# A fused softmax convolution and token mixer on one core: how the first load of x, the later loads, the zeros and the order of work are changed

## The chip, the cores and the metric

One core of one Trainium2 chip runs one program. The time is device microseconds of one launch, from the unprofiled runs; a separate profiled execution gives the trace. TensorE is PE in the profile (PEld its weight loads), VectorE is DVE, ScalarE is ACT, GpSimd is POOL, SyncE is SP. Loads and stores of the core share 16 DMA engines.

## What is computed

The input x has shape (8, 4224, 192) in fp32: 8 batches, 4224 tokens, 192 channels, in 8 heads of 24 channels. Two steps follow each other.

```python
# step 1: causal convolution over 7 tokens, one softmaxed filter per head
w = softmax(weight, axis=-1)                      # (8, 7)
y[b, s, h] = sum_k w[h, k] * x_pad[b, s + k, h]   # 6 zero rows ahead of each batch
# step 2: token mixing without a softmax, then an output projection
wq, wk = y @ w_q, y @ w_k                         # 192 -> 64 each
mixed  = (wq @ wk.T / 8) @ y                      # per batch, over all 4224 tokens
out    = relu(mixed) @ w_out                      # 192 -> 192, fp32
```

Since step 2 has no softmax, the kernel never forms the 4224 x 4224 matrix: it builds the Gram matrix y.T @ y of a batch (192 x 192), multiplies it with w_k, and applies the result to wq.

## The kernel before

**Tiles.** A batch is cut into 35 chunks (`NCC`) of 122 tokens (`CW`); a chunk is loaded as 128 rows, with the 6 tokens ahead of it. `XW` holds the chunks of all 8 batches in bf16 at once, so no load waits for a buffer. `Y`, `WQT` and the mixing weights `MSB`, `MBD` have two buffers; `RT` (relu results) has 3 and `OUT` (fp32 results, from which stores go) has 4.

**Stages of a batch**, each made by a function that adds operations to a list: `gen_conv` (matmuls of `XW` with the band matrix `BAND`, L391/L392, evacuated into `Y` at L671), `gen_transpose` and `gen_transpose_hi` (tokens to the free side, L395/L396 and L726), `gen_wq` (L751/L755), `gen_gram` (L787), `gen_mix_weights` (the small products behind a batch's Gram matrix), and `gen_mix` (mix_lo L878, mix_hi L890, relu L907/L908, fin_hi L935, fin_lo L391/L392 on `WOL`, evacuation L970, store L978 by SP). Most matmuls use 64 columns of the array and run in pairs side by side; mix_lo and fin_hi use 64 rows instead.

**Order.** `Planner.plan` takes the operations and simulates five engines with given durations; whenever an engine is free it places the ready operation with the lowest turn from the list `TURNS`, one number per operation. `STAY` is added to the turn of an operation that would change PE between 64 columns and 64 rows, and `HOLD` is how long PE waits for one that doesn't. The outcome is a fixed instruction stream for every engine, in which each instruction waits for semaphores; `tail` and `lands` tell the planner when a transfer is taken to have landed.

**The start.** DVE sets some tiles to zero (`zero_w` to `zero_m`, L410 to L422), POOL makes the identity, SP loads the 8 x 7 filters (L402). DVE then runs the chain of the softmax: wmx (L461), two subtractions, the exponential on ACT (L482), sum, reciprocal, `wtap`, `taps` (L494). PE spreads `taps` into PSUM in two halves of 512 columns, and ACT and DVE each evacuate one half into `BAND` (L527). The first convolution waits for both halves, for x, and for `zero_x`, `zero_x0`.

**Loads.** All loads of x go through POOL's queue, which turns fp32 into bf16 on the way (L565). Batch 0 comes in groups of 9, 9, 9 and 8 chunks, the later ones in groups of 18 and 17; a group is one large transfer, and the first and the last chunk of a batch have one of their own. POOL issues them one after the other without waiting for any landing. The mixing weights go by SP's queue (L587), behind the landing of the second group.

Of the kernel before, what the change touches and what calls it, by code (L numbers as in the profile page):

```python
# [13 lines left out]
    int(t) / 1000  # L14
    for t in """
# [56 lines left out]
class Op:  # L72


    n = 0
# [983 lines left out]
```

## Time and profile before

| what | value |
|---|---|
| median of 3 runs | 177.69 us (177.29 to 178.58) |
| the profiled execution's own time | 177.53 us |
| its span, first to last instruction | 175.7 us |
| PE busy | 157.1 us (89%), 3226 matmuls |
| ACT busy, DVE busy | 123.5 us (70%), 118.0 us (67%) |
| POOL's queue (loads of x) | 36128 packets, 13.61 MB |
| SP's queue (filters, weights, stores) | 12000 packets, 26.31 MB |
| instruction queue | 25 packets, 0.41 MB |

A line of the page's groups reads: line, engine, operation, tiles out<-in, shapes, count | busy time, mean of one in ns | idle time of the engine just before, and what ended it. In the timeline the columns are start, duration, engine, line, operation, tiles, shapes, count, and in brackets the idle time before with its releaser. "issue" as a releaser means that nothing which the profile shows was waited for. A line of waits reads: who waited, for whom, us in total, times, the longest. The bytes of POOL's queue are counted as written, in bf16.

### The profile page before, as it was taken

The page shows a single profiled execution, that of the slowest core. Times are in us where ns is not written, and L with a number is a line of the kernel's source. Part 1 is how long each engine was busy: PE and PEld are TensorE (multiplying, and loading weights), DVE is VectorE, ACT ScalarE, POOL GpSimd, SP SyncE. Part 2 cuts the span into 40 slices and gives each one's busy share as a digit, 9 for nine tenths or more (in the row PEclk, how much of TensorE's full clock was granted, in tenths as well). Part 3 has the DMA queues.
Part 4 walks back from the last instruction along what each step waited for, and adds up shares of the span by engine and source line. Part 5 has one row for each costly group of instructions (what it writes and reads, how often), then busy time and mean ns, then how long its engine had stood idle before and what let it go on. Part 6 is the DMA issues. An engine that isn't in the chain of part 4 may idle for free.

```text
span 175.7 us, 7099 instructions
## 1 busy us (share of the span) xinstructions
PE 157.1 (89%) x3226; PEld 121.7 (69%) x3226; DVE 118.0 (67%) x216; ACT 123.5 (70%) x206; POOL 30.3 (17%) x39
## 2 busy tenths in 40 slices
PE   0289799888999999899989979999999999999990
PEld 0179666776787787668778766878767777877550
DVE  6556587765766677586787738689688675765740
ACT  3243677597787948668648747888888896698980
POOL 7999452524230000000000000000000000000000
PEclk9999999999999999999999999999999999999995
DMA  3999999999999999999999999067283045987787
GB/s 30 162 189 186 205 191 193 191 196 277 193 279 194 286 309 268 343 250 243 304 264 282 237 194 348 24 244 297 103 343 127 4 175 216 356 347 309 265 303 262
DMA packets 48157, 40.36 MB, mean 230 GB/s; under 512 B 37632, under 2 KB 40960, under 8 KB 48128
## 3 DMA queue, kind: packets, MB, share of 16 engines
q0 software_dynamic: 36128, 13.61, 65.1%
q1 hardware_dynamic: 12000, 26.31, 40.9%
q8 instruction: 25, 0.41, 0.9%
q14 instruction: 4, 0.03, 0.1%
HBM read 27.56 MB, written 25.95 MB: 305 GB/s over the span
## 4 chain that ended last, share of the span: by engine, by line
PE 88%; issue 4%; DVE 3%; ACT 2%
PE ps L391 25%; PE ps L787 14%; PE ps L935 8%; PE ps L392 7%; PE ps L395 6%; PE ps L726 6%; PE ps L878 5%; PE ps L751 4%; PE ps L890 4%; PE ps L755 4%; PE ps L396 3%; ACT rt L907 1%; ACT out_sb L970 1%; DVE band L527 0%; DVE xw L416 0%
## 5 line engine op out<-in xcount | busy, mean ns | idle before, releaser
L970 ACT COPY out_sb<-ps 128x768 f32<-128x768 f32 (+1 forms) x46 | 34.7, 768 | 15.1 <-PE ps L392 11.3
L671 ACT CAST y<-ps 122x816 bf16<-122x816 f32 (+3 forms) x46 | 35.7, 791 | 13.2 <-PE ps L392 12.8
L907 ACT ACTIVATE rt<-ps 128x1024 bf16<-128x1024 f32 (+3 forms) x44 | 34.1, 800 | 6.4 <-PE ps L878 4.5
L787 PE MATMUL ps<-y 122*64 122x192 bf16 (+4 forms) x840 | 33.8, 222 | 2.2 <-issue 2.2
L970 DVE COPY out_sb<-ps 128x768 f32<-128x768 f32 (+1 forms) x26 | 21.6, 840 | 19.7 <-PE ps L392 18.5
L392 PE MATMUL ps<-wol,rt 128*64 128x192 bf16 x264 | 33.9, 255 | 1.0 <-issue 1.0
L787 PEld LDWEIGHTS ps<-y 122*64 122x64 bf16 (+1 forms) x840 | 31.1, 112 | 4.9 <-issue 2.8
L565 POOL DMA_DIRECT2D xw<-in_x_dram x34 | 29.9, 893 | 22.3 <-issue 21.5
L391 PE MATMUL ps<-wol,rt 128*64 128x192 bf16 x264 | 33.7, 255 | 0.0
L391 PE MATMUL ps<-xw,band 128*64 128x432 bf16 (+3 forms) x144 | 31.8, 335 | 1.5 <-DVE band L527 0.9
L392 PE MATMUL ps<-xw,band 128*64 128x432 bf16 (+3 forms) x144 | 32.1, 337 | 1.1 <-issue 1.1
L391 PEld LDWEIGHTS ps<-wol,rt 128*64 128x64 bf16 x264 | 24.1, 138 | 8.1 <-issue 2.0
L908 DVE TENSOR_SCALAR rt<-ps 128x512 bf16<-128x512 f32 (+3 forms) x36 | 23.6, 674 | 8.2 <-PE ps L878 7.6
L671 DVE CAST y<-ps 122x864 bf16<-122x864 f32 (+3 forms) x26 | 23.6, 912 | 8.0 <-PE ps L392 7.5
L698 DVE COPY ytl<-ps 128x976 bf16<-128x976 bf16 (+1 forms) x40 | 23.0, 591 | 3.9 <-PE ps L396 3.3
L392 PEld LDWEIGHTS ps<-wol,rt 128*64 128x64 bf16 x264 | 24.1, 138 | 1.2 <-issue 1.2
L396 PE MATMUL ps<-ident,y 122*64 122x122 bf16 x280 | 21.1, 219 | 0.0
L395 PE MATMUL ps<-ident,y 122*64 122x122 bf16 x280 | 21.0, 219 | 0.0
L935 PE MATMUL ps<-woh,rt 64*128 64x192 bf16 x264 | 20.4, 250 | 0.2 <-ACT rt L907 0.2
L395 PEld LDWEIGHTS ps<-ident,y 122*64 122x64 bf16 x280 | 18.1, 112 | 2.0 <-issue 0.5
L726 PE MATMUL ps<-ident,y 122*64 122x122 bf16 (+1 forms) x344 | 17.1, 220 | 1.3 <-DVE y L671 0.7
L396 PEld LDWEIGHTS ps<-ident,y 122*64 122x64 bf16 x280 | 17.7, 112 | 0.0
(95 smaller groups left out, 218.8 us busy)
## 6 DMA issues: line engine op xcount, KB each, us to landing
out_dram<-out_sb SPq DMA_DIRECT2D x28, 768.0 KB, 5.1
xw<-in_x_dram POOLq DMA_DIRECT2D x7, 816.0 KB, 33.2
xw<-in_x_dram POOLq DMA_DIRECT2D x7, 768.0 KB, 33.7
out_dram<-out_sb SPq DMA_DIRECT2D x8, 384.0 KB, 3.3
xw<-in_x_dram POOLq DMA_DIRECT2D x2, 432.0 KB, 8.3
out_dram<-out_sb SPq DMA_DIRECT2D x8, 96.0 KB, 4.3
xw<-in_x_dram POOLq DMA_DIRECT2D x1, 384.0 KB, 5.2
xw<-in_x_dram POOLq DMA_DIRECT2D x8, 45.8 KB, 25.0
```

Source lines behind the costliest of these rows:

```text
L391: e.matmul(out[0:64], lhsT[:, 0:64], rhs, **k)
L392: return e.matmul(out[64:128], lhsT[:, 64:128], rhs, **k)
L395: e.transpose(out[0:64], in_[:, 0:64], identity)
L396: return e.transpose(out[64:128], in_[:, 64:128], identity)
L565: lambda e, op, part=part: e.dma_start(*part),
L671: return e.copy(dst, src) if op.engine == "ACT" else e.tensor_copy(dst, src)
L726: last = e.transpose(ps[64 * i : 64 * i + HI, o : o + w], Y[0:w, yb, c, LO:D], IDENT[0:w, 0:w])
L787: mm = e.matmul(bank(GB)[p : p + 64, o : o + z - r], Y[0:w, yb, c, r : r + 64], Y[0:w, yb, c, r:z], start=st, stop=end, skip_group_check=True,
L907: return e.activation(dst, src(), AF.Relu)
L908: return e.tensor_scalar(dst, src(), 0.0, None, op0=ALU.max)
L935: last = e.matmul(bank(op.bank + a)[:, o : o + D], RT[64 * a : 64 * a + HI, slot, 2, i:n:nt], WOH[64 * a : 64 * a + HI, :], start=i == q, ...
L970: return e.copy(dst, src) if op.engine == "ACT" else e.tensor_copy(dst, src)
```

## The change

1. The first nine chunks of batch 0 are loaded in fp32 by SP's queue, in two transfers, into `RAW`, a part of `OUT`. Three ACT copies of three chunks each cast them into `XW`, placed behind the exponential. The six zero rows ahead are now set in `RAW` (`zero_r`); `zero_x0` covers the other seven batches. The first users of `OUT` wait for the casts.
2. POOL's first load is thereby the second group of batch 0. From batch 1 on, each group is loaded in four large pieces of 4 or 5 chunks, each with a semaphore of its own, and each large piece waits on POOL for the landing of the large transfer three before it. The mixing weights wait for the third group's landing.
3. `zero_w`, `zero_q`, `zero_yt`, `zero_k` and `zero_m` come behind `taps` on DVE.
4. `BAND` is made in four parts of 256 columns, on ACT, DVE, ACT, DVE.
5. `TURNS`, `STAY`, `HOLD` and some durations that the planner works with are new, and so is the order of all engines' streams.

```diff
--- before.py
+++ after.py
@@ -11,58 +11,94 @@
 
 
 TURNS = [
-    int(t) / 1000
+    int(t) / 1e6
     for t in """
...
 """.split()
 ]
 
@@ -108,9 +144,9 @@
     LAT = {"PE": 240.0, "ACT": 145.0, "DVE": 140.0, "POOL": 150.0, "SP": 0.0}
     SWITCH = 145.0
 
-    STAY = 0.865
-
-    HOLD = 1
+    STAY = 1.305216
+
+    HOLD = 41.263032
 
     def __init__(self, nbank, first_bank):
         self.ops = []
@@ -412,7 +448,11 @@
     zero_s = add("DVE", lambda e, op: e.memset(STEPT[:, :], 0.0), 150, vt=-8.9)
     eps = add("DVE", lambda e, op: e.memset(WEX[:, 0, :, 7], 1e-9), 100, vt=-9.4)
     zero_e = add("DVE", lambda e, op: e.memset(WEX[:, 1, :, 7], 0.0), 100, vt=-9.4)
-    zero_x0 = add("DVE", lambda e, op: e.memset(XW[0 : KC - 1, :, 0, :], 0.0), 800, vt=-8.8)
+
+    NRAW = 9
+    RAW = OUT[:, :, :, :, :].rearrange("p s t q d -> p (s t q d)")[:, 0 : NRAW * D].rearrange("p (c d) -> p c d", d=D)
+    zero_r = add("DVE", lambda e, op: e.memset(RAW[0 : KC - 1, 0, :], 0.0), 130, vt=-9.3)
+    zero_x0 = add("DVE", lambda e, op: e.memset(XW[0 : KC - 1, 1:, 0, :], 0.0), 750, vt=-8.8)
@@ -426,7 +466,7 @@
         lambda e, op: e.affine_select(
             IDENT[:, :], IDENT[:, :], [[-1, 128]], ALU.is_equal, 0.0, base=0, channel_multiplier=1
         ),
-        1250,
+        700,
         needs=[one],
         vt=-9,
     )
@@ -455,7 +495,7 @@
     own = add(
         "DVE",
         lambda e, op: e.tensor_reduce(OWN[:, :], IDENT[:, :].rearrange("p (k i) -> p i k", i=16), AX.X, ALU.add),
-        200, needs=[ident], vt=-8.92)
+        200, needs=[ident], vt=-7.83)
 
 
     mx = add("DVE", lambda e, op: e.tensor_reduce(WMX[:, :], WT_F[:, :, :], AX.X, ALU.max), 150, needs=[load_w], vt=-8)
@@ -501,52 +541,79 @@
     )
     taps.needs.append(own)
 
+    for zero in (zero_w, zero_q, zero_yt, *zero_k, zero_m):
+        zero.after.append(taps)
+
 
     bands = []
-    for q0, engine in ((0, "ACT"), (4, "DVE")):
+    for q0, engine in ((0, "ACT"), (2, "DVE"), (4, "ACT"), (6, "DVE")):
 
         def spread(e, op, q0=q0):
             last = None
-            for q in range(q0, q0 + 4):
+            for q in range(q0, q0 + 2):
                 last = halves(
                     e,
                     bank(op.bank)[:, (q - q0) * 128 : (q - q0 + 1) * 128],
                     STEPT[0:112, 112 - 16 * q : 240 - 16 * q],
                     TAPS[0:112, :, :].rearrange("p i h -> p (i h)"),
                     start=q == q0,
-                    stop=q == q0 + 3,
+                    stop=q == q0 + 1,
                     skip_group_check=True,
                 )
             return last
 
-        fill = add("PE", spread, 260, needs=[taps, stept], banks=1, vt=-7 + 0.1 * q0)
+        fill = add("PE", spread, 200, needs=[taps, stept], banks=1, vt=-7 + 0.1 * q0)
 
         def band(e, op, q0=q0, fill=fill):
-            dst = BAND[:, :, 16 * q0 : 16 * q0 + 64]
-            src = bank(fill.bank).rearrange("p (j h) -> p h j", h=H)
+            dst = BAND[:, :, 16 * q0 : 16 * q0 + 32]
+            src = bank(fill.bank)[:, 0 : 32 * H].rearrange("p (j h) -> p h j", h=H)
             return e.copy(dst, src) if op.engine == "ACT" else e.tensor_copy(dst, src)
 
-        bands.append(add(engine, band, 550, drains=fill, vt=-6.9))
+        bands.append(add(engine, band, 340, drains=fill, vt=-6.9))
 
 
     load = {}
-    at = [5000.0]
+    S_RAW = semaphore("s_raw")
+    big_loads = []
+
+    LANDS = [0.0, 6600.0, 8700.0, 10900.0]
+
+    raw = []
+    for dst, src in (
+        (RAW[:, 1:NRAW, :], bass.AP(x_t, (CW - KC + 1) * D, [[D, 128], [CW * D, NRAW - 1], [1, D]])),
+        (RAW[KC - 1 : 128, 0, :], bass.AP(x_t, 0, [[D, CW], [1, D]])),
+    ):
+        raw.append(
+            add("SP", lambda e, op, dst=dst, src=src: e.dma_start(dst, src), 450, dma=("raw", S_RAW, 16), tail=2200, vt=-8.9)
+        )
+        raw[-1].lands = 3700.0
+    load[0, 0] = []
+    for c in range(0, NRAW, 3):
+
+        def cast_x(e, op, c=c):
+            dst, src = XW[:, 0, c : c + 3, :], RAW[:, c : c + 3, :]
+            return e.copy(dst, src)
+
+        load[0, 0].append(
+            add("ACT", cast_x, 540, needs=[*raw, zero_r], after=[ex], vt=-7.2 + 0.01 * c)
+        )
 
     def gen_load(b, gi):
-        sem = semaphore(f"s_x{b}_{gi}")
         cs = groups_of(b)[gi]
         parts = []
         base = b * S * D
         full = [c for c in cs if 0 < c < NCC - 1]
         if cs[0] == 0:
             parts.append((XW[KC - 1 : 128, b, 0, :], bass.AP(x_t, base, [[D, CW], [1, D]])))
-        n = len(full)
-        parts.append(
-            (
-                XW[:, b, full[0] : full[0] + n, :],
-                bass.AP(x_t, base + (CW * full[0] - KC + 1) * D, [[D, 128], [CW * D, n], [1, D]]),
+        pieces = 4 if b else 1
+        for k in range(pieces):
+            some = full[len(full) * k // pieces : len(full) * (k + 1) // pieces]
+            parts.append(
+                (
+                    XW[:, b, some[0] : some[0] + len(some), :],
+                    bass.AP(x_t, base + (CW * some[0] - KC + 1) * D, [[D, 128], [CW * D, len(some)], [1, D]]),
+                )
             )
-        )
         if cs[-1] == NCC - 1:
             rows = S - (CW * (NCC - 1) - KC + 1)
             parts.append(
@@ -556,24 +623,27 @@
                 )
             )
 
-        at[0] += len(cs) * 260.0
         load[b, gi] = []
         for k, part in enumerate(parts):
-            first = (b, gi) == (0, 0) and part[0].shape[1] > 1 and len(part[0].shape) == 3
+            first = (b, gi) == (0, 1) and part[0].shape[1] > 1 and len(part[0].shape) == 3
+
+            gate = big_loads[-3:][:1] if b else []
             op = add(
                 "POOL",
                 lambda e, op, part=part: e.dma_start(*part),
                 900,
-                needs=[zero_x] if cs[-1] == NCC - 1 else [],
+                needs=[*([zero_x] if cs[-1] == NCC - 1 else []), *gate],
                 after=[] if first else [ident],
-                dma=(f"x{b}_{gi}", sem, 16),
+                dma=(f"x{b}_{gi}_{k}", semaphore(f"s_x{b}_{gi}_{k}"), 16),
                 vt=-10 if first else -4 + b + gi * 0.1 + 0.02 * k,
             )
-            op.tail = 1500.0
-            op.lands = at[0]
+            op.tail = 1500.0 if b == 0 else 3200.0
+            op.lands = LANDS[gi] if b == 0 else 0.0
+            if len(part[0].shape) == 3:
+                big_loads.append(op)
             load[b, gi].append(op)
 
-    for gi in range(len(groups_of(0))):
+    for gi in range(1, len(groups_of(0))):
         gen_load(0, gi)
 
 
@@ -586,7 +656,7 @@
                 pairs.append((WHI[p : p + HI, cols], bass.AP(t, LO * n, [[n, HI], [1, n]])))
             return [(e.dma_start(d, s), 16) for d, s in pairs]
 
-        return add("SP", emit, 1700, needs=load[0, 1], dma=(name, semaphore(f"s_{name}"), 16 * 3), tail=4000, vt=vt)
+        return add("SP", emit, 1700, needs=load[0, 2], dma=(name, semaphore(f"s_{name}"), 16 * 3), tail=4000, vt=vt)
 
     load_q = gen_weight("wq", wq_t, DH, QS, -3.0)
     load_k = gen_weight("wk", wk_t, DH, KS, -2.9)
@@ -868,7 +938,7 @@
         n_rt += 1
         n_out += 1
         free = rt_read.get(n_rt - 1 - NRT, [])
-        ofree = store_of[n_out - 1 - NOUT] if n_out > NOUT else []
+        ofree = store_of[n_out - 1 - NOUT] if n_out > NOUT else load[0, 0]
         vt = b + 1.2 + t0 / S * 0.95
         nt = n // 128
 
```

136 rows, old and new, of the table TURNS are left out of this document.

## The prediction

> **What bounds the kernel now.** I read the table of stages first (busy time of each engine in stretches that I chose: up to the first convolution, the rest of the half-speed start, the load phase in two parts, the phase after the last load, the end).
>
> ```profile
> core 0: us, PE busy (x) PEld busy (x) DVE busy (x) ACT busy (x) POOL busy (x), PEclk, DMA share, GB/s
> 0.00:8.76 8.76, 1.39 (x18) 0.98 (x19) 5.33 (x24) 2.34 (x4) 7.58 (x14) 1.00 0.88 96
> 8.76:15.10 6.34, 5.63 (x82) 5.25 (x84) 2.87 (x6) 2.07 (x4) 6.34 (x8) 1.00 1.58 188
> ...
> 36.00:105.00 69.00, 65.46 (x1398) 51.72 (x1394) 47.37 (x79) 49.33 (x81) 5.40 (x7) 1.00 1.36 259
> 105.00:163.00 58.00, 58.00 (x1208) 44.02 (x1202) 42.37 (x74) 48.04 (x79) 0.00 (x0) 1.00 0.58 224
> ```
>
> PE carries the middle: 65.46 of 69.00 us while x is loaded, all of 58.00 after that. So three things can move the end: when PE starts, what makes it idle in the load phase, and how long its own stream is. Second, PE's waits in 18 to 104 us (there is none in 106 to 163):
>
> ```profile
> PE ps L787 <- issue: 2.2, 2, 1.3
> PE ps L392 <- issue: 2.1, 2, 1.1
> PE ps L391 <- issue: 0.6, 1, 0.6
> PE ps L726 <- issue: 0.5, 1, 0.5
> ```
>
> These are six idles, 5.4 us together, in which no other engine was waited for: the instruction itself was not there. Third, the DMA queues in 18 to 103 us:
>
> ```profile
> q0 software_dynamic: 29063, 10.96, 107.6%
> q1 hardware_dynamic: 4074, 9.93, 33.2%
> q8 instruction: 14, 0.23, 1.0%
> ...
> xw<-in_x_dram POOLq DMA_DIRECT2D x4, 816.0 KB, 45.5
> ```
>
> q0 is POOL's queue with all x loads; its loads land 45.5 us after issue, so the backlog is never empty. q8 brings PE's instructions in pieces of 16 KB, some 128 matmuls each. The packet records put these pieces 6.09 to 6.91 us apart from 18.01 to 100.72 us, mean 6.36 us (13 steps), and each of the six idles ends 2.3 to 2.5 us after such a piece started (18.01 and 20.48, 37.69 and 40.15, 100.72 and 103.09). When q0 ends at 105.7 us the idles end with it. I read this as instruction supply slowed by q0. Stores show the same delay: issued at 54.54 us, first packet at 58.25; issued at 142.10, first packet about 0.8 us later. Fourth, the head, from the timeline:
>
> ```profile
> 3.02 0.11 DVE L417 MEMSET wqh<- 128x64 uint32 x1
> ...
> 4.70 0.15 DVE L461 TENSOR_REDUCE wmx<-wt_f 128x8 f32<-128x56 f32 x1
> ...
> 5.39 0.30 ACT L482 ACTIVATE wex<-wex 128x112 f32<-128x112 f32 x1 [1.25 <-DVE wex L473]
> ...
> 6.47 0.29 DVE L494 TENSOR_TENSOR taps<-own,wtap 128x128 bf16<-128x128 f32 x1
> ...
> 7.50 0.58 ACT L527 CAST band<-ps 128x512 bf16<-128x512 f32 x1 [1.82 <-PE ps L392]
> ...
> 7.93 0.69 DVE L527 CAST band<-ps 128x512 bf16<-128x512 f32 x1 [1.16 <-PE ps L392]
> ```
>
> The first convolution at 8.76 us waits for DVE's band (8.62), not for x, which had landed by 6.5 us. DVE is busy without a break from 2.2 us to wmx at 4.70, and its weights had landed at 3.7. PE then runs at half speed, although the clock column says 1.00: a pair of 216-column matmuls every 0.18 us here, a pair of 408 columns every 0.17 us later; it is at full speed from 15.1 us.
>
> **The change part by part.** The profiled run took 177.53 us, 1.83 us more than its span of 175.7, and 0.16 us below the median of 177.69; the sum starts from 177.53.
>
> *Zeros moved behind taps.* Three memsets from 3.02 to 3.42 and three from 4.28 to 4.70 leave the chain: 0.82 us. Added is the zero for RAW, 6x192 f32, about 0.20 us (stept's 128x120 took 0.16); zero_x0 has seven batches of eight, 0.70 x 1/8 = 0.09 us less. Net 0.71 us: wmx at 3.99, just behind its weights; exp ends at 4.98 instead of 5.69, taps at 6.05 instead of 6.76. The six memsets now run on DVE at 6.05 to 6.9 us, under the spread matmuls; without that cover they would cost 0.82 us. Behind them on DVE stand its two bands.
>
> *Four bands of half size.* Half of 128x512 is 0.58 - 256/1200 = 0.37 us on ACT and 0.69 - 256/960 = 0.42 us on DVE. The spread ends at 7.18 us, DVE's bands by 7.84.
>
> *Raw x by SP, cast by ACT.* The trace has no fp32 load of x. SP issues it at 1.2 us behind the weights; those took 1.0 us from issue to first packet, so it starts at 2.2. It has 1024+122 packets. Lower bound: at the full rate of q0 (245 packets in half a microsecond) 2.35 us, plus 0.25 for the semaphores: 4.8 us. Upper bound: q0's packets start at 3.2 us, and an equal share to the end gives 2.2 + 2298/490 + 0.3 = 7.2; at the 7.5 packets per us and engine that the weights got beside q0 in 15 to 18 us it is about 9.0. I take 5.7, nearer the lower end, since q0 began slowly (26 and 80 packets in its first two half microseconds). The three casts are ACT's first work behind exp, and ACT's two bands queue behind them, so all of PE waits for them. One 128x576 cast, from 432 columns at 519 ns and 816 at 840: 0.64 us; three overlapped, 1.8. Landing 5.7, casts to 7.55, two bands to 8.29, convolution at 8.43 us: 0.33 us earlier. Bounds by the landing: 4.8 gives 7.98 (-0.78, DVE's bands then decide), 7.2 gives +1.2, 9.0 gives +3.0. Break-even is a landing at 6.0.
>
> *The convolutions behind it.* The second group's load is now POOL's first; 2298 packets at 490 per us have landed at about 7.2 us (the second group before: 10.5). PE can run 32 convolution matmuls in one go; before, it did 16, then idled 0.70 us from 10.42 on. That idle goes: 0.7 us. Uninterrupted work from 11.11 to 15.1 was what preceded full speed, 4.0 us; from 8.43 that would be 12.4, and the work left then, 1.6 us, takes half. I count 0.5 of these 0.8 us. Bounds of both: 0 and -1.5; taken: -1.2.
>
> *Loads in pieces, each waiting for the third before it.* From batch 1 on, 56 large loads of 4 or 5 chunks instead of 14 of 16 or 17. POOL's issue time is hidden (30 us busy, nothing else to do). A piece is 32 packets per engine, so at most about 100 are queued where before several hundred were; in the 1.9 us from an issue to its first packet (1.30 to 3.2) the queue drains some 57, so it swings between about 10 and 70, 40 in the mean. The delay of 3.7 us in a store's start, against 0.8, is 2.9 us or about 87 packets at 30 per us; half of that goes. If instruction pieces shorten alike, the six idles shrink. Bounds 0 (three pieces still fill the queue) and -5.4; I take half, -2.7. Behind each POOL wait stand only later loads, and x keeps its place in SBUF for all batches, so loads still run ahead: 30 packets per us and engine carry a batch (8 pieces, 256 packets) in under 9 us, and PE takes 20.
>
> By the Trainium skill, Runtime: NRT & Kernel Launch, section Instruction fetch mechanics, code arrives in 16 KiB blocks through the sequencer's own DMA queue, and the cost of a block is mostly hidden. The 16 KB pieces agree with this trace, the hidden cost doesn't where q0 is full (5.4 us). By that rule this term would be 0 and the sum 174.9.
>
> *Order searched anew.* All PE instructions are the same kinds and counts (3226 matmuls). In the new stream PE goes between 64-row and 128-row tiles 94 times instead of 106. Over the 106 in the trace a change of this sort delays the next matmul by 96 ns (median; the row pair 167.56 to 167.75 us, where 0.08 is usual, shows one): 12 x 0.096 = -1.1 us, as PE is the bound. ACT and DVE work, counted with the durations of these rows: ACT 131 to 127 us plus casts, DVE 124 to 128; both have room. New small waits can't be read from counts: 0, bounds +-2.
>
> *The end.* PE ends at 170.8, the last store at 174.8, stores running at 370 GB/s from 168 on. The same 384 KB stores follow the last batch in both: 0, bounds +-0.7.
>
> Sum: 177.53 - 0.33 - 1.2 - 2.7 - 1.1 = 172.2 us.
>
> **The rivals.** (1) *The pieces change nothing for instruction supply*: three pieces are 1.2 MB in flight, enough for the 87 packets. For it: q0 gets a new piece before it is empty. Against: half the time it would be shorter. Then the 5.4 us stay, and half of the saved switches is lost in waiting for code: 177.53 - 1.53 - 0.55 = 175.5 us. The rule above gives nearly the same time. (2) *All idles in the load phase go*, and the start gains its full 1.5: 177.53 - 0.33 - 1.5 - 5.4 - 1.1 = 169.2. For it: PE was busy 58.00 of 58.00 us without q0. (3) *Slower: the software queue crowds out the hardware queues even when it is shallow.* Place: the raw load on SP, with ACT's bands stuck behind its casts. For it: the weights got 7.5 packets per us and engine against q0's 25. Against: q0 is empty until 3.2 us. Price: landing at 9.0, +3.0 us, no gain in clock, idles kept, half the switches: 177.53 + 3.0 - 0.55 = 180.0. It decides against the change from a landing past 6.0 us if nothing else is gained, and by over 1% from about 8.4.
>
> The Trainium skill, DMA: Bandwidth & Descriptors, section Rules for kernel authors, says that spreading DMAs over SP, ACT and GpSimd brings no bandwidth, since all share 16 engines and interleave; only issue time is saved. That speaks for rival 3, and the weights at 15 us (q0 down to 25.2 from 31.0 packets) agree.
>
> **How the numbers follow.** Chances: forecast 0.47, rival 1 0.21, rival 2 0.16, rival 3 0.16. A measurement of this kernel tells about 1% (1.8 us) from no change, so faster means below 175.9. Nearly all of the forecast, all of rival 2 and about half of rival 1 lie there, less a little for unread waits: 0.70. Same gets the rest of rival 1 and of the forecast's edge, 0.13; slower 0.17. The forecast's own range is 169.5 to 175; for 8 in 10 I go from 168.5 (rival 2 and some of the order's bound) to 178.5, which leaves out most of rival 3.
>
> **What would show it.** Right: the first convolution near 8.4 us with ACT's casts from 5.7; full speed before 14 us; x loads landing some 4 to 6 us after issue; PE's idles on issue below 3 us in all; instruction pieces under 5.5 us apart while q0 runs. Wrong: casts that start behind 6.5 us; idles on issue still near 5 us; PE waiting for ACT, DVE or an x load in the middle, where before it waited for none.

## The result, and the profile after

The changed kernel takes 192.7 us (median of 4 runs, 191.87 to 195.18) against 178.09 for the kernel before beside it: a ratio of 1.081 [1.074, 1.088], 8% slower. Ratios, here and below, leave out executions more than 1.5% above the fastest of the same kernel; medians take in all. The prediction of 172.2 was wrong, also in its sign, and 192.7 lies far outside its range. The profiled execution took 191.87 us with a span of 190.4, so 14.7 us are to be found against the span of 175.7 before.

First the table of stages, as before (columns: the stretch, its length, busy time of each engine, PE's granted clock, DMA, GB/s):

```profile
core 0: us, PE busy (x) PEld busy (x) DVE busy (x) ACT busy (x) POOL busy (x), PEclk, DMA share, GB/s
0.00:12.34 12.34, 1.38 (x19) 0.96 (x20) 5.62 (x26) 4.12 (x8) 4.93 (x11) 1.00 1.04 167
...
18.00:104.00 86.00, 72.76 (x1549) 57.17 (x1546) 53.90 (x91) 52.14 (x92) 35.92 (x50) 0.94 1.18 199
104.00:140.00 36.00, 34.90 (x746) 27.93 (x742) 26.66 (x44) 26.00 (x43) 10.71 (x15) 1.00 1.13 231
```

The first convolution starts at 12.34 us instead of 8.76. In the load phase PE is busy 72.76 of 86.00 us, where 65.46 of 69.00 had been, and the phase lasts to 140 instead of 105.7. The clock column is 0.94. The waits of PE from 13 us on, and POOL's over the whole span (who waited, for whom, us, times, longest):

```profile
PE ps L427 <- DMA xw<-in_x_dram: 12.0, 3, 7.2
PE ps L857 <- issue: 0.7, 1, 0.7
```

```profile
POOL xw L633 <- DMA xw<-in_x_dram: 78.5, 38, 6.2
```

The idles on issue are nearly gone (0.9 us in all, from 5.3), and in their place stands what was not there at all: 12.0 us in which PE waits for x, three times (2.87, 1.98 and 7.20 us). POOL in turn spends 78.5 us waiting for landings. The DMA queues in 18 to 138 us (packets, MB, share of 16 engines; then the loads' KB and median us from issue to landing):

```profile
q0 software_dynamic: 30557, 11.29, 85.6%
...
xw<-in_x_dram POOLq DMA_DIRECT2D x46, 192.0 KB, 5.8
```

The queue of the loads is no longer full (85.6%, from 107.6%), and it carries 17.1 packets per us and engine from 18 to 100 us, where it had carried 21.8 before. The longest wait in the timeline of PE, and the slices of the page (4.76 us each; clock in tenths):

```profile
73.14 0.27 PE L431 MATMUL ps<-ident,y 122*64 122x122 bf16 x2
80.61 0.52 PE L427 MATMUL ps<-xw,band 128*64 128x408 bf16 x1 [7.20 <-DMA xw<-in_x_dram]
```

```profile
PE   0249989999679954099999999899999999999970
...
PEclk9999999999999999559999999999999999999998
```

Some 2.5 us into that wait the clock falls to half, and it stays there from 75.9 to 86.2 us by the clock records. The head, in the timeline:

```profile
1.26 0.95 SPq L587 DMA_DIRECT2D out_sb<-in_x_dram  x2
...
4.94 0.21 DVE L501 TENSOR_REDUCE wmx<-wt_f 128x8 f32<-128x56 f32 x1 [0.93 <-DMA wt_f<-in_weight_dram]
...
6.77 0.29 DVE L534 TENSOR_TENSOR taps<-own,wtap 128x128 bf16<-128x128 f32 x1
...
9.93 1.82 ACT L595 CAST xw<-out_sb 128x576 bf16<-128x576 f32 x3 [3.95 <-DMA out_sb<-in_x_dram]
...
11.65 0.64 ACT L570 CAST band<-ps 128x256 bf16<-128x256 f32 x2
12.34 0.13 PEld L427 LDWEIGHTS ps<-xw,band 128*64 128x64 bf16 x1 [4.40 <-ACT band L570]
```

wmx waits 0.93 us for the filters, the casts start at 9.93, ACT's two bands stand behind them, and PE waits 4.16 us for the bands.

The 14.7 us add up on PE's records: first convolution +3.6 (8.76 to 12.34); idle behind it +8.6 (6.3 to 14.9, waits for x +12.0, issue -4.4, the rest +1.0); busy +1.9 (155.8 to 157.7, the same 3226 matmuls at half clock for longer); from PE's end to the span's end +0.7 (4.8 to 5.5).

### The profile page after: what moved, and what is told of

It reads as the page before. It is cut to its first block, busy times and chain, and to the rows that moved or that the text cites. A ratio compares the mean times of both kernels' runs of the same rounds, so it can differ in the third digit from the quotient of the medians.

```text
span 190.4 us, 7172 instructions
## 1 busy us (share of the span) xinstructions
PE 159.0 (84%) x3226; PEld 124.5 (65%) x3226; DVE 122.9 (65%) x220; ACT 122.5 (64%) x208; POOL 54.4 (29%) x79
## 4 chain that ended last, share of the span: by engine, by line
PE 44%; DMA 43%; POOL 4%; issue 3%; ACT 2%; DVE 2%; POOLq 0%; DVEq 0%; ACTq 0%
DMA xw<-in_x_dram 36%; PE ps L427 12%; DMA out_dram<-out_sb 7%; PE ps L857 6%; PE ps L1005 6%; POOL xw L633 3%; PE ps L796 3%; PE ps L428 3%; PE ps L948 3%; PE ps L431 2%; PE ps L821 2%; PE ps L960 2%; PE ps L825 2%; PE ps L432 2%; ACT out_sb L1040 2%
## 5 line engine op out<-in xcount | busy, mean ns | idle before, releaser
L633 POOL DMA_DIRECT2D xw<-in_x_dram x74 | 54.0, 734 | 81.9 <-DMA xw<-in_x_dram 78.5
L741 ACT CAST y<-ps 122x864 bf16<-122x864 f32 (+3 forms) x46 | 34.9, 784 | 30.8 <-PE ps L428 30.2
L427 PE MATMUL ps<-xw,band 128*64 128x408 bf16 (+3 forms) x144 | 32.2, 349 | 16.4 <-DMA xw<-in_x_dram 12.0
L1040 ACT COPY out_sb<-ps 128x768 f32<-128x768 f32 (+1 forms) x41 | 30.9, 764 | 12.9 <-PE ps L428 10.8
L1040 DVE COPY out_sb<-ps 128x768 f32<-128x768 f32 (+1 forms) x31 | 26.6, 860 | 15.9 <-PE ps L428 13.2
L857 PE MATMUL ps<-y 122*64 122x128 bf16 (+4 forms) x840 | 33.4, 223 | 0.7 <-issue 0.7
L428 PE MATMUL ps<-xw,band 128*64 128x408 bf16 (+3 forms) x144 | 32.4, 351 | 0.0
L427 PE MATMUL ps<-wol,rt 128*64 128x192 bf16 x264 | 31.8, 255 | 0.0
L428 PE MATMUL ps<-wol,rt 128*64 128x192 bf16 x264 | 31.7, 255 | 0.0
L427 PEld LDWEIGHTS ps<-xw,band 128*64 128x64 bf16 x144 | 15.2, 121 | 19.7 <-issue 13.8
L427 PEld LDWEIGHTS ps<-wol,rt 128*64 128x64 bf16 x264 | 23.5, 138 | 6.9 <-issue 2.1
L803 DVE COPY yth<-ps 128x512 bf16<-128x512 bf16 (+1 forms) x40 | 14.6, 376 | 11.4 <-PE ps L796 11.3
L431 PEld LDWEIGHTS ps<-ident,y 122*64 122x64 bf16 x280 | 18.4, 112 | 1.5 <-ACT wqt L841 0.4
```

The source lines that it names most:

```text
L427: e.matmul(out[0:64], lhsT[:, 0:64], rhs, **k)
L428: return e.matmul(out[64:128], lhsT[:, 64:128], rhs, **k)
L431: e.transpose(out[0:64], in_[:, 0:64], identity)
L633: lambda e, op, part=part: e.dma_start(*part),
L741: return e.copy(dst, src) if op.engine == "ACT" else e.tensor_copy(dst, src)
L857: mm = e.matmul(bank(GB)[p : p + 64, o : o + z - r], Y[0:w, yb, c, r : r + 64], Y[0:w, yb, c, r:z], start=st, stop=end, skip_group_check=True,
```

## The experiments

The theory (T): the waits ahead of the loads hold q0 to a rate that PE's stream outruns, whatever the order, and this is most of the loss; the late raw load is a smaller part. The first rival (P): the new order takes x in lumps and the waits merely show it. The kernels keep the instruction streams of the kernel that they are made from, except for what the edit names. The edits are shown in short; those to waits and loads are made behind the plan, so that the order stays.

**1. The waits taken out.** The pieces, the head and the order stay.

```diff
+    for op in planner.order:
+        if op.engine == "POOL" and op.dma is not None:
+            op.needs = [x for x in op.needs if x not in big_loads]
```

> The changed kernel with every landing wait of POOL's loads taken out; the pieces, all streams and all other waits stay. Theory T (the changed kernel lost 12.05 us of PE waiting for x and some 4 us of half clock behind the longest wait to the gate of three pieces, and 3.6 us to the late first convolution, and gained some 4.4 us of instruction idles): PE's waits for x in the middle fall from 12.05 us to below 1 and the clock stays up, the backlog returns and with it 4 to 5 us of idles on issue; time 192.7 - 12 - 4 + 4 = 181 us (178 to 183). Rival P (the splitting into 56 pieces, or the new order that wants x earlier, is what starves PE): PE still waits over 8 us for x and the time stays above 187.

Measured: 180.85 us (180.79 to 180.91), ratio 1.020 [1.017, 1.023]. PE waits for no x, and q0 ends at 101.6 us in place of 140.1. So the waits cost 11.85 of the 15 us in this order, and P fell. PE's waits from 13 us on show what is left:

```profile
PE ps L1005 <- DVE out_sb L1040: 2.2, 1, 2.2
PE ps L431 <- issue: 1.7, 1, 1.7
PE ps L427 <- issue: 0.9, 2, 0.5
```

The idles on issue are 3.5 us here, and a wait of 2.2 us for a buffer of results is new. It was in no sum of the prediction.

**2. The raw load mended.** The first chunk's transfer of 122 rows ends late: on the timeline's clock the sixteen semaphore writes of the eight-chunk transfer are all in by 7.34 us, and of the other there are only two late ones, at 9.22 and 9.90 (the expectation below has these times some 0.35 us too early; the casts start at 9.93). By the Trainium skill, DMA: Bandwidth & Descriptors, section "Why a DMA increments its semaphore by 16 and not by 1", a transfer is spread over the largest number of engines up to 16 that divides its outer dimension; 122 gives 2. The trace agrees (16 + 2 semaphore writes behind 5.9 us, and 13 raw packets per half microsecond from 7.5 us on, where there had been 219 at 5.0). So the transfer was cut in 112 and 10 rows:

```diff
-e.dma_start(RAW[KC - 1 : 128, 0, :], bass.AP(x_t, 0, [[D, CW], [1, D]]))
+e.dma_start(RAW[KC - 1 : KC + 111, 0, :], bass.AP(x_t, 0, [[D, 112], [1, D]]))
+e.dma_start(RAW[KC + 111 : 128, 0, :], bass.AP(x_t, 112 * D, [[D, CW - 112], [1, D]]))
```

> The changed kernel with the raw load of chunk 0 (122 rows) split into 112 and 10 rows; nothing else. Theory T (the 122 rows go over two DMA engines only: the records show two late semaphore writes at 8.87 and 9.59 us, where the eight-chunk part had landed at 6.90): ACT's casts start near 7.2 instead of 9.93 us, the first convolution near 9.7 instead of 12.34, time 192.7 - 2.5 = 190 us. Rival Q (POOL's queue crowds the raw load out, as rival 3 of the prediction said): the casts still start behind 9 us and the time stays within 0.5 us.

```profile
8.00 1.82 ACT L601 CAST xw<-out_sb 128x576 bf16<-128x576 f32 x3 [1.79 <-DMA out_sb<-in_x_dram]
```

The casts start 1.93 us earlier and the first convolution at 10.41; both are later than expected (7.2 and 9.7), since the last semaphore write still comes at 7.98. The time is 191.7, only 1.0 below the changed kernel: PE still waits 10.5 us for x. A start that comes earlier meets the same loads.

**3. The wait moved from three to eight large loads back.**

```diff
+            op.needs = [x for x in old if x not in big_loads]
+            if op.needs != old and n >= 8:
+                op.needs.append(big_loads[n - 8])
```

> The changed kernel with each load waiting for the large load eight before it instead of three. Theory T: eight pieces in flight carry x fast enough, PE's waits for x below 1 us; the backlog is about 8 x 32 packets per engine, so if instruction supply is slowed by any backlog above some 90 packets, the idles on issue are those of the kernel without gates (4 to 5 us), time about 181 us as in e1_no_gates. Rival R (instruction supply gets worse in proportion to the backlog): idles on issue of 1 to 3 us, time 1.5 to 3 us below e1_no_gates. Rival P: PE still waits over 8 us for x.

Measured: 183.16 us, no wait for x, idles on issue 3.05, and the steps of the instruction queue 6.44 us in the mean, as without waits (6.41). A backlog of eight pieces is as deep as an endless one for the instructions. The 2.3 us above run 1 come at two places, read by the start of each matmul in both profiled executions. By 17 us run 3 is 1.4 us behind, since PE reaches full speed at about 18 us instead of 15.2; 0.8 of that is left at 30 us. And PE idles 2.08 us at 82.9 on the buffer of results and then has half its clock from 86.5 to 89.9, 1.6 us more, which run 1's profiled execution, with the same idle, did not.

**4. Runs 1 and 2 together**, to see what the earlier start is worth where nothing waits for x.

```diff
+            op.needs = [x for x in op.needs if x not in big_loads]
+e.dma_start(RAW[KC - 1 : KC + 111, 0, :], bass.AP(x_t, 0, [[D, 112], [1, D]]))
```

> Both edits: no landing waits, and chunk 0 of the raw load in 112 and 10 rows. Theory T: the two losses add: e1_no_gates less 2.5 us, about 178.5 us, as fast as the kernel before within 1.5 us. Rivals P and Q: above 185 us.

Measured: 180.63 us, ratio 1.019 [1.004, 1.034]; first convolution at 10.36. The medians differ by only 0.2 us from run 1, but the two executions here (179.51 and 181.75) lie 2.2 us apart, so the gain stays open. In the profiled one PE starts 2.0 us earlier than in run 1's and is still 1.7 us ahead at its last matmul.

**5. POOL's head put back.** Run 1 with the first nine chunks by POOL's queue, cast on the way, ahead of IDENT; no ACT casts.

```diff
+    raw[0].emit = lambda e, op: e.dma_start(XW[:, 0, 1:NRAW, :], ...)
+    raw[1].emit = lambda e, op: e.dma_start(XW[KC - 1 : 128, 0, 0, :], ...)
+    order[i : i + 1] = [raw[0], ident, raw[1], x01]      # on POOL
```

> The changed kernel without the waits ahead of the loads, and with the first nine chunks loaded and cast by POOL's queue again, ahead of IDENT, as the kernel before does it; ScalarE's casts are gone. What stays of the change: the pieces, the four bands, the zeros behind the taps, the new order. Theory T (the late raw load, wmx behind the weights that share a queue with it, and the waits for landings are all that costs): first conv 8.0 to 8.4 us in place of 12.38 without the waits, wmx at 4.1 or earlier, so 4.2 us less than 180.85: 176.6 (175.8 to 177.6). Rival O (the new order is itself worse, by conv to end of PE some 1 us more than the kernel before): 178 to 179, although the first conv is at 8.2.

Measured: 180.71 us, ratio 1.020 [1.017, 1.022], although the first convolution is at 7.86. T fell here, and O stood in its direction, with more than the 1 us that it named: head and waits are not all. Read matmul by matmul, the profiled execution is 4.5 us ahead of run 1's at the 20th, 1.9 at the 40th, 0.5 at the 100th, 1.3 at the 300th (run 1 has the longer idle on issue), 0.7 at the 1400th, and 0.9 behind at the 1500th. The first loss is the second group of x (timeline of PE):

```profile
10.82 0.39 PE L427 MATMUL ps<-xw,band 128*64 128x216 bf16 x1 [2.38 <-DMA xw<-in_x_dram]
```

The second is the start at half speed: full speed comes at about 16 us, in run 1 at 15.2. The third stands behind the wait for a buffer of results (the chain of waits from 74 to 88 us, then two stretches of the table of stages):

```profile
74.89 7.24 DMA out_dram<-out_sb
...
82.22 0.97 DVE out_sb L1040
...
83.24 0.52 PE ps L1005 x5
```

```profile
84.50:87.90 3.40, 3.40 (x41) 2.98 (x39) 1.76 (x3) 1.87 (x3) 0.00 (x0) 0.50 1.56 194
87.90:92.00 4.10, 4.10 (x101) 3.33 (x99) 3.30 (x7) 2.78 (x7) 0.00 (x0) 1.00 1.26 303
```

A store takes 7.24 us to land, DVE's evacuation into its buffer waits for that, PE waits for DVE, and the clock is halved for 3.4 us. Run 1 has the same wait (2.15 us) without the halved clock. Three of this run's six executions, with a mean clock of 0.990 to 0.995 against 0.982 in the profiled one, took 180.27 to 180.79 us, so the halved clock is not the whole loss there; where theirs lies is not shown.

**6. The zeros alone, in the kernel before.**

```diff
+    i = order.index(taps) + 1
+    order[i:i] = moved      # the six memsets, taken out of their old places
```

> The kernel before with one part of the change alone: six memsets of DVE moved behind taps. The prediction's step (net 0.71 us, wmx from 4.70 to 3.99): first conv 8.0 to 8.1 in place of 8.76, and 0.6 to 0.8 us off 177.3: 176.6. Rival: the chain is set by IDENT or by the weights' landing before that, so wmx moves by less than 0.4 and the time by less than 0.4; or the first conv comes earlier and the later idles on instruction supply take it back, time 177.2.

Measured: 177.07 against 177.51 us, ratio 0.997 [0.994, 1.000]. The first convolution comes at 8.14 instead of 8.76, and wmx at 3.74, with only the filters ahead of it in SP's queue:

```profile
3.74 0.45 DVE L461 TENSOR_REDUCE wmx<-wt_f 128x8 f32<-128x56 f32 x1
...
5.85 0.29 DVE L494 TENSOR_TENSOR taps<-own,wtap 128x128 bf16<-128x128 f32 x1
```

The step was right in the head; some 0.4 of its 0.6 us reach the end.

**7. and 8. The pieces in the kernel before, with and without the waits.** Order and head of before; the 14 large loads of batches 1 to 7 cut in four.

```diff
+        for k in range(4):
+            piece = copy.copy(op)                        # own semaphore, a quarter of the chunks
+            piece.needs += big[-3:][:1]                  # run 7 only
+            big.append(piece)
```

> The kernel before, in its own order and with its own head, with the large loads of batches 1 to 7 cut in four pieces, each behind the landing of the large load three before. Theory T (the waits hold the loads to some 18.3 us a batch whatever the order): the last load lands near 138 to 142 in place of 105.7, PE waits for x by 7 us or more in all, time 184 to 191, 187 taken; idles on instruction supply under 2. Rival P (the waits bite only because the new order takes x in lumps): PE waits for x under 2 us, and fewer idles on instruction supply bring 173 to 178.

> The same pieces without the waits. The prediction took half of the idles on instruction supply away for the pieces with their waits; its first rival took none. Theory T (only fewer outstanding loads, not smaller ones, help the instruction supply): steps of the instruction queue 6.2 to 6.5 us as before, idles 5 to 5.6, time 177.3 (176.5 to 178). Rival: pieces alone change the queue's turn, steps under 5.5, idles under 4, time 175 to 176.

Run 7: 188.36 us, ratio 1.060 [1.057, 1.064]. PE's waits from 13 us on:

```profile
PE ps L391 <- DMA xw<-in_x_dram: 6.9, 2, 4.5
PE ps L787 <- issue: 2.2, 1, 2.2
PE ps L391 <- DVE rt L908: 1.1, 1, 1.1
```

q0 ends at 137.8 us; the clock is halved three times (3.4, 6.8 and 3.4 us). In the order before, too, the waits cost 10.9 us (11.2 beside run 8, which has the pieces without the waits), so it is not the new order that makes them bite. The idles on issue are still 3.5, not under 2. The largest, 2.19 us, ends at 131.1, when q0 still runs. Run 8: 177.16 us, ratio 0.998 [0.996, 1.001]. Cutting the loads changes nothing by itself.

**9. Five buffers of results.** Run 5, same streams.

```diff
-    NOUT = 4
+    NOUT, PLANNED = 5, 4    # the plan is made with 4; only the waits for stores then go five back
```

> The kernel with the first nine chunks by POOL's queue and no waits ahead of the loads, now with five buffers for results in place of four, in the same order. Theory T (the new order's loss against the order before is a result that waits for the store four before it: 2.1 us of idle PE near 81, and 3.4 us of half clock right behind it): that idle and the half clock go, 3.5 to 4 us off 180.7: 177.0 (176.3 to 177.8), as the kernel before. Rival O (the order loses in many small places, and the wait moves to the next engine when the buffer is there): less than 2 us off, 179 or more.

Measured: 178.31 us, ratio 1.004 [1.002, 1.007]; PE waits for no result:

```profile
PE ps L432 <- issue: 1.6, 1, 1.6
PE ps L797 <- issue: 0.9, 1, 0.9
PE ps L858 <- issue: 0.7, 2, 0.4
```

2.4 us off, between the two expectations and nearer the rival's (less than 2) than T's (3.5 to 4). T's mechanism holds as far as the wait goes, which is gone from PE's waits; its amount was too high. What is left is 0.4% above the kernel before.

**10. and 11. Shallower waits that might starve nothing.** The kernel before with the zeros of run 6 and the pieces of run 7, each behind the large load five or four before.

```diff
-            piece.needs += big[-3:][:1]
+            piece.needs += big[-5:][:1]      # run 11: big[-4:][:1]
```

> The kernel before with the six zeros behind taps and the loads of batches 1 to 7 in four pieces, each behind the landing of the large load five before. Theory T (the queue carries a batch in 13.4 us when it is full, and three pieces out carry one in 18.3; five should reach 13.5 to 15, so PE waits for no x, but the queue is then as full as with eight out, where the instruction queue's steps were 6.4): idles on instruction supply 4.5 to 5.5, time 176.8 (176 to 178), as without the waits. Rival (a backlog of five already frees the instruction queue): idles under 3.5, time 174 to 175.5.

> The same with the wait for the large load four before. Theory T: a batch in some 14 to 16 us, steps of the instruction queue down to 5 at the least, idles on instruction supply 3.5 to 5; PE waits for x by 0 to 2 us near 27 or 40, where three pieces out cost 2.4 and 4.5; time 177.5 (175.5 to 180). Rival: idles fall under 3 and no wait for x is left: 174 to 175.5, the prediction's gain for the pieces with another depth.

Five: 176.96 us in the median of six, but from 173.98 to 183.01, where run 6 stayed within 175.95 and 178.6. The profiled execution, 175.29, has idles on issue of 2.66, against 5.58 in run 6's, so the rival's expectation held in that execution. Four: 181.0 us (178.33 to 182.79), with 1.7 us of waiting for x, 4.7 on issue and a halved clock. At four the ratio is 1.011 [1.006, 1.016]. Beside run 6's median a depth of five buys 1.8 and 3.1 us in two executions of six, on which alone its ratio of 0.985 [0.981, 0.989] rests, and loses 5.9 in another; why they differ stays open, since only one of them has a trace.

**12. The late head with five buffers.** Run 1 with run 9's edit; beside run 9 it differs only in the head.

```diff
-    NOUT = 4
+    NOUT, PLANNED = 5, 4    # as in run 9
```

> The changed kernel with its own head (first nine chunks as fp32 by SyncE's queue, cast by ScalarE; first conv at 12.4 us), no waits ahead of the loads and five buffers for results. Beside it stands the same with POOL's head, first conv 7.86, at 178.31. Theory T (most of the 4.5 us is given back, since PE with the early head waits for the second group of x until 10.9 to 11.9 anyway, and 1.4 us is left at the first conv of batch 1): 179.7 (179 to 180.5). Rival H (the whole of the later start comes through to the end): 182 to 183.

Measured: 179.99 us (179.27 to 180.54). Of the 4.4 us by which PE starts later (12.28 against 7.86) 1.7 reach the end in the medians. In the two profiled executions 2.8 are left at PE's last matmul: 1.6 go where run 9's PE waits for the second group.

**13. and 14. The wait six loads back**, in the kernel before with its zeros moved, and in run 9.

```diff
+            piece.needs += big[-6:][:1]      # run 14: op.needs.append(big_loads[n - 6])
```

> The kernel before with the zeros behind taps and the loads in pieces, each behind the landing of the large load six before. Five before gave a profiled execution of 175.29 with idles of 2.66 on instruction supply, but others of its executions up to 183. Theory T (at six PE waits for no x in any execution, and the backlog is nearly as deep as without waits): idles 3 to 5, times close together, 176.5 (175.3 to 177.3). Rival: the gain of the best executions at five stays and the long ones go: 174 to 175.3.

> The new order with POOL's head and five buffers (178.31 without waits), with the wait for the large load six before. Theory T: no wait for x, idles on instruction supply 3 to 4.3 in place of 4.28, 177.8 (176.8 to 178.8). Rival: idles under 2.5, 175 to 176.5, which would beat the kernel before with the new order.

177.46 us (176.3 to 179.56), ratio 0.998 [0.996, 1.001], and 178.41 (177.05 to 179.76), ratio 1.004 [1.002, 1.007], idles on issue 4.6 and 5.9 in the profiled executions. At six the waits buy nothing in either order.

**The account in times** (one way through the runs; other ways give other parts: the fifth buffer is worth 2.4 us between runs 5 and 9, 0.9 between runs 1 and 12):

| step | us |
|---|---|
| kernel before | 177.5 |
| new order, bands, zeros, pieces, five buffers, POOL's head (run 9) | 178.31 |
| raw load by SP, cast by ACT (run 12) | +1.7 = 179.99 |
| four buffers, as the change has it (run 1) | +0.9 = 180.85 |
| waits for landings (the changed kernel) | +11.85 = 192.7 |

No run's median is more than 0.3% below the kernel before (runs 6, 8 and 10), and run 10's lower ratio rests on two executions. What the new order and the four bands do apart from each other is not shown.

## Why the prediction was wrong, point by point

**"Loads still run ahead", the step that failed.** The prediction took 30 packets per us and engine, a batch in under 9 us, for a queue that each landing has to open again, and priced the waits between 0 and -5.4: no loss was in its bounds. Even without the waits 30 was too high: it is what the full queue carries with nothing beside it, while the prediction's own row (29063 packets in 85 us) gives 21.4, some 13 us for a batch of 282 packets per engine. With the waits, a load waits for the landing of the third before it, and the small loads of a batch stand in the same line. A piece lands 5.6 us after its issue in the median, and three pieces of 32 packets per engine in 5.6 us are the 17.1 packets per us and engine that were measured. The slow ones took longer: the one issued at 68.72, beside stores of 768 KB, held up the one at 76.76. Over the whole stretch a batch takes 18.3 us (the seven from 12.05 to 140.06). The conclusion "and PE takes 20" was off too: in the trace before, the first convolutions of batches 1 and 7 are at 23.5 and 129.7, 17.7 us a batch. So the loads were not twice as fast as PE, but slower. Run 1 (waits out, -11.85 us) and run 7 (waits into the old order, +10.9) show it from both sides. The sentence "Behind each POOL wait stand only later loads" was true and of no help: behind the later loads stands PE.

**"Half of that goes", the gain.** The changed kernel has 0.9 us of idles on issue, but the time gains nothing by it: without the waits there are 3.5 in the same order, the pieces alone leave the time as it was (run 8), and the waits at three in the old order leave 3.5. PE cannot wait for code while it waits for x. The mechanism itself was right, which shows in the place of the instruction pieces in PE's stream. Ahead of its first wait for x, the changed kernel has six pieces behind 15 us, and each starts 57 to 200 PE instructions earlier in the stream than the same piece in run 1. At the 40 instructions per us that PE begins in the middle, that is 1.4 to 5 us. With eight loads out (run 3) the second to eleventh piece start within 7 instructions of run 1's. So rival 1 (nothing for instruction supply) was right for the time, for the pieces alone and for a depth of eight, but not for a depth of three.

Two marks that the prediction had set for being right came true, loads landing in 4 to 6 us and idles on issue below 3. Three did not: the first convolution (12.34), full speed (17.9) and instruction pieces under 5.5 us apart (7.0 in the mean). Of those set for being wrong, casts behind 6.5 us and PE waiting for x in the middle came. The spacing of the pieces could not tell: PE's 6500 instructions (3226 matmuls, as many weight loads) came in 25 pieces, some 260 each, so at 40 per us they stand 6.4 us apart at PE's own pace, and in the trace before they are 6.25 us apart behind q0's end too. The prediction's reading of that spacing as slowed supply was wrong, though the supply was late.

**Raw landing, 5.7 us taken, bounds 4.8 and 9.0.** It came at 9.90, outside the bounds, and in the main not for the reason of rival 3: the raw load was ahead of q0, whose packets start only at 5.45. Rival 3 had place and price almost right (landing 9.0, +3.0 us; measured first convolution +3.6), while run 2 shows that most of the lateness behind 7.3 us comes from the 122 rows on two engines. Two things stay open: q0's packets ran beside those two engines' from 5.45 us on, and no run tells that share apart; and with the rows cut the landing is still at 7.98 and the first convolution 2.0 us behind the predicted 8.43. The price at the end was too high in both: run 12 gives 1.7 (2.8 in the profiled executions), since PE with an early head waits for the second group.

**wmx at 3.99.** It was 4.94, and taps ended at 7.06 instead of 6.05. The raw load shares SP's queue with the filters, whose last semaphore write moved from 3.75 to 4.91 us. In run 6, with the filters alone there, wmx came at 3.74 and the first convolution 0.63 us earlier; the 0.71 of the prediction was about right where the queue was left alone.

**Idle 0.70 and the earlier clock, -1.2.** The second group's large load landed at 11.24 us, not at 7.2. Its convolutions did run on without a gap in the changed kernel, but from 13.8 us on, and the full clock came at 17.9 instead of 15.1.

**Switches, -1.1.** PE's busy time behind the first convolution is 155.8 us before and 155.2 in run 9, with 6.3 and 6.0 us of it in the start at half speed: at most 0.5 of the 1.1 is there. **New small waits, 0 +-2.** In the changed kernel the waits for anything but x and instructions grew by 1.0 us, inside the bound. Without the waits for landings the order loses more: one buffer of results, 2.1 us of idle and at times 1.6 for the clock (runs 5 and 9: 2.4 us in the time), just outside it. **The end, 0 +-0.7:** +0.7, at the bound.

**The clock behind a long idle** was in no step. In the changed kernel it was halved for 10.2 us, in 5.6 of which PE worked, so some 2.8 us were lost.

## What to carry to other kernels

Before a wait for a landing is put ahead of a load, work out the rate that it leaves: pieces outstanding, divided by issue to landing in the traced phase, against what the consumer takes in the same phase; a rate seen with a full queue says nothing about one that is opened by landings. A depth that doesn't bind (six or eight here) buys nothing either, so the window between starving and useless may be too narrow to use. And part of a head start is lost where its consumer meets the next thing that it needs, here 1.6 of 4.4 us at the second group of x.

## What was not expected of the hardware

- The granted clock is halved in steps of 3.41 us: 3.41 in the profiles of runs 3, 5, 7, 8 and 11, 6.83 around an idle of 4.47 us (run 7), 10.24 around one of 7.20. Idles of 2.08 to 2.41 us took one step in six cases (runs 3, 5, 8 and 11, run 7 twice). Idles of 2.11 to 2.15 us took none in runs 1, 4 and 14, nor did one of 2.87 in the changed kernel. The Trainium skill, TensorE: Matmul & The Clock Gate, Part 1: The HAM clock gate (the "warmup" mystery), gives a free-running window of 3.4 us and an idle window as the condition; the step agrees, but here idles well below that length were enough in six of the ten cases.
- A transfer of 122 rows on SP's queue had two late semaphore writes, at 9.22 and 9.90 us, one of 128 rows on the same queue sixteen, the last at 7.34.
- POOL's first load packets start at 5.45 us with the raw load in flight, where they had started at 3.02 without it (the prediction read 3.2), although POOL issued its load at 1.3 in both.
